# Batch 0's attention first and alone with filler matmuls, the weight fold behind tile 0

## Chip, cores, metric

One NeuronCore of one Trainium2 chip. The metric is device time in microseconds (us) of one execution; lower is better. Times quoted are medians of several runs, profiles are of one run each.

## The reference

Strided sparse attention over 8 batches, 8 heads, 576 positions, head size 64, then a feed-forward part without a nonlinearity:

```python
attn = softmax(mask(q @ k.T / 8)) @ v          # heads 0-3: local mask, 4-7: strided mask
x = attn.transpose(0, 2, 1, 3).reshape(4608, 512)
a = x @ w1;  b = x @ w2                         # 512 x 1024 each
out = ((a * b) @ w3) @ w_out                    # 1024 x 1024, 1024 x 512
```

There is no nonlinearity between w3 and w_out, so the kernel multiplies them once: w34 = w3 @ w_out, the **fold**. A **tile** is 512 tokens (nine of them), a batch is 576 tokens.

## The kernel before

Weights and q, k, v come as float32 through five 8 KB staging buffers (`stgp`) and are cast to float16 by POOL or ACT. Here the parts that matter, with cuts marked `...`:

```python
def load_w3(g, engs="pp"):
    st = stgp.tile([P, 2, DF], FP32, tag="stg")
    nc.sync.dma_start(st, ...)
    for i in range(2):
        t = ffn.tile([P, DF], FP16, tag="w3n", bufs=4)    # eight chunks, four buffers
        w3n[2 * g + i] = t
        copy(engs[i], t, st[:, i])

def load_vL(b):
    vt = v16L[b % 2]
    ...
    for pr in (bass.ds(32, 32), bass.ds(64, 64)):
        nc.gpsimd.tensor_copy(out=vt[pr, :, :, 0:D], in_=...)
    # the "shift copy": 32 partitions moved to another 32
    nc.vector.tensor_copy(out=vt[0:32, :, 1:LT, 0:D], in_=vt[96:P, :, 0:LT - 1, 0:D])

def fold_tr(jc): ...      # 8 transposes of one w3 chunk, copies by DVE and ACT
def fold_mm(jc): ...      # two halves of 4 matmuls each: one block of w34

# attention of batch b, pair p of heads, as a stream of short steps:
#   ph_T (transpose q, k)  ph_R (their remainders)  ph_S (scores, exp, mask)
#   ph_PV (times v, normalise)  ph_T2 (transpose back into xT)

def host(units, upto, lead=0):     # emit dense units, the stream's steps between them
    ...
```

```python
load_w3(0, "pa"); load_wo(0); load_wo(1); load_qk(0); load_rest(0)
load_w3(1); load_vL(0); load_w3(2); load_vS(0); load_w3(3)
load_w12(0); load_w12(1)
load_qk(1); ...                                   # batch 1
fold_tr(0)
host(fold, batch_end[0], lead=3)                  # fold hosts batch 0's attention
load_qk(2); ...
host(ab_halves(0), pos[0] + 8, lead=9)            # tile 0: a and b
host(o_halves(0), batch_end[1])                   # tile 0: out, hosts batch 1
for tch in range(1, 9): ...                       # tile t hosts batch t + 1
```

PE runs in the order written. On the other engines the framework's scheduler orders the instructions, and each then runs strictly in that order.

## Time and profile before

| | before |
|---|---|
| median of 4 runs | 301.46 us (300.86 to 304.81) |
| span of the profiled run | 302.7 us (that run took 304.5 us) |
| first scores of batch 0 | 29.2 us |
| tile 0's first b matmul | 53.6 us |
| tile 1's first matmul | 90.3 us |
| from there to the end | 212.4 us |

The last row is dense PE work (PE is busy for 206.2 of these 212.5 us). Nearly all the slack lies ahead of tile 1, so the table is read by its second to last row: whatever a change does in the loading, fold and tile 0 stages shows there. The profiled run was taken apart from the four and is as slow as the slowest of them, which matters when sums from the trace are added to the median.

One detail of that trace will matter. Batch 1's shift copy on DVE, and POOL's casts at that time (timeline of the kernel before; start, length, engine, line, operation, out and in, and in brackets the wait before it):

```profile
68.86 2.47 POOL L169 CAST t<-st 128x1024 f16<-128x1024 f32 x2 [2.47 <-DMA st<-in_k_dram]
...
70.45 1.22 DVE L186 COPY v16L<-v16L 32x1280 f16<-32x1280 f16 x1
71.27 0.87 POOL L177 CAST t<-st 128x512 f16<-128x512 f32 x1
```

### The profile page before, as it was taken

To read this page: it belongs to the slowest core of one execution; us is meant where nothing else is said; L and a number is where in the kernel's file an instruction comes from. 1 tells how busy PE (TensorE), PEld (TensorE's weight loads), DVE (VectorE), ACT (ScalarE), POOL (GpSimd) and SP (SyncE) were. 2 spreads that over 40 slices of the span, in tenths; PEclk is the share of its full clock that TensorE was granted. 3 is DMA by queue.
4 is the path that set the end of the run, shared out by engine and by line. 5 is a ranking of instruction groups with operands and counts; after the bars stand their busy time and mean duration, and the time that the engine had idled before them with its cause. 6 is when DMAs were issued, how large, how long until landed. Compare 5 with 4: busy or idle time off the path is not lost.

```text
span 302.7 us, 5967 instructions
## 1 busy us (share of the span) xinstructions
PE 271.2 (90%) x2401; PEld 142.3 (47%) x2401; DVE 168.1 (56%) x345; ACT 149.6 (49%) x272; POOL 96.2 (32%) x99
## 2 busy tenths in 40 slices
PE   1728887996889999999999999999999999999995
PEld 0305554343455455555555555555554555444442
DVE  1100776226777884887678568847755774340430
ACT  3414568263675546445555565555455444433332
POOL 4358525665235462656119306110000000000000
PEclk9975999799999999999999999999999999999999
DMA  7999999999189988999899460020012002002003
GB/s 256 361 292 267 342 382 268 186 292 144 38 266 223 208 216 214 345 168 226 226 207 287 132 167 2 2 106 35 1 38 106 0 2 104 35 2 111 28 2 140
DMA packets 55612, 48.63 MB, mean 161 GB/s; under 512 B 28192, under 2 KB 44576, under 8 KB 55584
## 3 DMA queue, kind: packets, MB, share of 16 engines
q1 hardware_dynamic: 50400, 38.80, 52.7%
q10 hardware_dynamic: 5184, 9.44, 8.8%
q8 instruction: 19, 0.31, 0.5%
q14 instruction: 9, 0.07, 0.1%
HBM read 38.80 MB, written 9.44 MB: 159 GB/s over the span
## 4 chain that ended last, share of the span: by engine, by line
PE 75%; ACT 8%; DVE 6%; SPq 4%; DMA 3%; issue 3%; POOL 0%; ACTq 0%
PE ops L339 22%; PE bps L325 20%; PE aps L316 18%; PE ps L218 5%; PE xps L272 5%; DVE ptm L259 3%; DMA st<-in_moe_w_dram 3%; PE sps L252 3%; ACT pte L257 3%; SPq L163 2%; SPq L175 2%; PE ps L288 2%; ACT xT L295 2%; ACT osb L350 1%; DVE kT L72 1%
## 5 line engine op out<-in xcount | busy, mean ns | idle before, releaser
L316 PE MATMUL aps<-xT,w1h 128*128 128x512 f16 x288 | 76.1, 382 | 2.5 <-ACT xT L295 2.3
L319 ACT COPY asb<-aps 128x512 f32<-128x512 f32 x72 | 42.2, 586 | 71.4 <-PE aps L316 70.0
L327 DVE TENSOR_TENSOR abt<-bps,asb 128x512 f16<-128x512 f32 x72 | 49.5, 687 | 49.1 <-PE bps L325 48.4
L325 PE MATMUL bps<-xT,w2h 128*128 128x512 f16 x288 | 74.9, 383 | 0.0
L339 PE MATMUL ops<-w,abt 128*128 128x512 f16 x288 | 70.7, 379 | 0.0
L169 POOL CAST t<-st 128x1024 f16<-128x1024 f32 x32 | 34.1, 1094 | 33.5 <-PE ps L218 14.7
L257 ACT ACTIVATE pte<-sps 128x576 f16<-128x576 f32 (+1 forms) x64 | 38.4, 650 | 6.7 <-PE sps L252 6.5
L280 DVE TENSOR_TENSOR xqs<-xps,rcp 96x384 f16<-96x384 f32 (+1 forms) x64 | 39.6, 619 | 2.0
L325 PEld LDWEIGHTS <-w2h 128*128 128x128 f16 x288 | 25.7, 98 | 30.3 <-issue 6.0
L350 ACT COPY osb<-ops 128x512 f32<-128x512 f32 x36 | 21.1, 586 | 31.6 <-PE ops L339 31.6
L70 ACT COPY qT<-ps 128x512 f16<-128x512 f16 (+1 forms) x48 | 22.9, 481 | 27.8 <-PE ps L218 21.8
L316 PEld LDWEIGHTS <-w1h 128*128 128x128 f16 x288 | 25.4, 98 | 22.8 <-issue 1.1
L339 PEld LDWEIGHTS <-abt 128*128 128x128 f16 x288 | 24.9, 98 | 23.4
L185 POOL CAST v16L<-st 32x1536 f16<-32x1536 f32 (+1 forms) x16 | 24.0, 1497 | 27.7 <-DMA st<-in_v_dram 17.8
L272 PEld LDWEIGHTS <-ptm 72*128 72x128 f16 (+1 forms) x448 | 21.2, 97 | 23.0 <-DVE ptm L259 9.3
L259 DVE TENSOR_TENSOR ptm<-pte,maskL 128x576 f16<-128x576 f16 x32 | 17.5, 548 | 16.1 <-ACT pte L257 15.6
L259 DVE TENSOR_TENSOR ptm<-pte,maskS 72x576 f16<-72x576 f16 x32 | 21.7, 687 | 8.5 <-ACT pte L257 8.3
L196 POOL CAST v16S<-st 72x1024 f16<-72x1024 f32 x16 | 17.1, 1083 | 25.7 <-PE xps L272 14.6
L72 DVE COPY kT<-ps 128x512 f16<-128x512 f16 (+1 forms) x36 | 18.8, 535 | 11.2 <-ACT qT L70 11.1
L339 PE MATMUL ops<-woh,w3T 128*128 128x512 f16 x64 | 20.4, 454 | 3.1 <-POOL woh L74 2.0
L218 PE MATMUL ps<-id,t 128*128 128x128 f16 x256 | 20.3, 223 | 2.8 <-POOL t L169 2.8
L218 PEld LDWEIGHTS <-t 128*128 128x128 f16 x256 | 17.1, 100 | 11.3 <-POOL t L169 3.3
(52 smaller groups left out, 185.4 us busy)
## 6 DMA issues: line engine op xcount, KB each, us to landing
out_dram<-osb ACTq DMA_DIRECT2D x36, 256.0 KB, 2.0
st<-in_moe_w_dram SPq DMA_DIRECT2D x8, 1024.0 KB, 12.1
st<-in_q_dram SPq DMA_DIRECT2D x8, 1024.0 KB, 8.9
st<-in_k_dram SPq DMA_DIRECT2D x8, 1024.0 KB, 13.4
st<-in_v_dram SPq DMA_DIRECT2D x8, 576.0 KB, 10.0
st<-in_v_dram SPq DMA_DIRECT2D x8, 512.0 KB, 10.4
st<-in_moe_w_out_dram SPq DMA_DIRECT2D x2, 1024.0 KB
st<-in_q_dram SPq DMA_DIRECT2D x8, 128.0 KB, 11.2
```

Source lines behind the costliest of these rows:

```text
L169: nc.gpsimd.tensor_copy(out=t, in_=sts[nm][:, 4 * grp:4 * grp + 4].rearrange("p h c d -> p c h d"))
L218: pe(nc.tensor.transpose(ps[:, i, c * P:(c + 1) * P], src[:, c, h0:h0 + 2].rearrange("p h d -> p (h d)"), id16))
L257: nc.scalar.activation(out=pte[0:kr], in_=sps[0:kr, :, 0:288], func=AF.Exp, bias=0.0, scale=scale)
L259: nc.vector.tensor_mul(ptm[0:kr, 0:576].rearrange("p (a x) -> p a x", x=w), pte[0:kr].rearrange("p h (a x) -> p (h a) x", x=w), _ap(mk, 0, ...
L272: pe(nc.tensor.matmul(xps[:, h, i * 65:(i + 1) * 65], ptm[0:kr, c0:c0 + P], vt[0:kr, 2 * (s.hp % 2) + h, g * m + i, :], start=True, stop=T ...
L280: nc.vector.tensor_mul(xqs[0:w, 0:m].rearrange("p i h d -> p h i d"), xv[:, :, :, 0:D], _ap(rcp, 0, [[rp, w], [4, 2], [1, m], [0, D]]))
L316: pe(nc.tensor.matmul(aps, w1h[:, ci, bass.ds(jc * P, P)], xT[ci][:, tok], start=(ci == 0), stop=(ci == KM - 1)))
L319: nc.scalar.copy(out=asb, in_=aps)
L325: pe(nc.tensor.matmul(bps, w2h[:, ci, bass.ds(jc * P, P)], xT[ci][:, tok], start=(ci == 0), stop=(ci == KM - 1)))
L327: nc.vector.tensor_mul(abts[tch][:, jc, :], bps, st["asb"])
L339: pe(nc.tensor.matmul(st["ps"], lhs(ci), rhs(ci), start=(ci == 0), stop=(ci == KF - 1)))
L350: nc.scalar.copy(out=osb, in_=ps)
```

## The change

Intent: let batch 0's attention, which needs only q, k, v, start as soon as they land, so that tile 0's a and b (dense work) start early; put the fold behind them, where it can host batch 1's attention. While batch 0's attention runs alone, two 512-column matmuls of an identity before each step ("filler") are to keep PE's clock up.

```diff
--- before.py
+++ after.py
@@ -156,7 +156,7 @@
 
     x16 = {}
 
-    def load_qk(b):
+    def load_qk(b, engs="pp"):
         sts = {}
         for nm, ten in (("q", q), ("k", k)):
             st = stgp.tile([P, H, 4, D], FP32, tag="stg")
@@ -164,9 +164,9 @@
                               ten[b, :, 0:NM].rearrange("h (p c) d -> p h (c d)", c=4))
             sts[nm] = st
         for grp in range(2):
-            for nm in "qk":
+            for nm, eng in zip("qk", engs):
                 t = qkp.tile([P, 4, 4, D], FP16, tag=f"{nm}{grp}")
-                nc.gpsimd.tensor_copy(out=t, in_=sts[nm][:, 4 * grp:4 * grp + 4].rearrange("p h c d -> p c h d"))
+                copy(eng, t, sts[nm][:, 4 * grp:4 * grp + 4].rearrange("p h c d -> p c h d"))
                 x16[(b, nm, grp)] = t
 
     def load_rest(b):
@@ -412,38 +412,44 @@
                 pos[0] += 1
 
 
+
+    def spin():
+        ps = psF.tile([P, NT], FP32, tag="f", name="spin")
+        for i in range(2):
+            pe(nc.tensor.matmul(ps, id16, _ap(id16, 0, [[id16.ap[0][0], P], [0, 4], [1, P]]),
+                                start=True, stop=True))
+
+    load_qk(0, "pa")
+    load_rest(0)
+    load_vL(0)
+    load_vS(0)
+    load_w12(0)
+    load_w12(1)
     load_w3(0, "pa")
     for g in range(2):
         load_wo(g)
-    load_qk(0)
-    load_rest(0)
-    load_w3(1)
-    load_vL(0)
-    load_w3(2)
-    load_vS(0)
-    load_w3(3)
-    load_w12(0)
-    load_w12(1)
+    for g in range(1, 4):
+        load_w3(g)
     load_qk(1)
     load_rest(1)
     load_vL(1)
     load_vS(1)
 
-    fold = []
-    fold_tr(0)
+    fold = [lambda: fold_tr(0)]
     for jc in range(KF):
         h0, h1 = fold_mm(jc)
         fold.append(h0)
         if jc + 1 < KF:
             fold.append(lambda jc=jc: fold_tr(jc + 1))
         fold.append(h1)
-    host(fold, batch_end[0], lead=3)
+    ALONE = batch_end[0]
+    host([spin] * ALONE, ALONE)
     load_qk(2)
     load_rest(2)
     load_vL(2)
     load_vS(2)
-    host(ab_halves(0), pos[0] + 8, lead=9)
-    host(o_halves(0), batch_end[1])
+    host(ab_halves(0) + fold[0:8], pos[0])
+    host(fold[8:] + o_halves(0), batch_end[1])
     for tch in range(1, NTILE):
         units = ab_halves(tch) + o_halves(tch)
         if tch + 1 < B:
```

> **What bounds the kernel now.** I read the busy times first, then a table of stretches, the chain that ended last, the PE timeline of the first 90 us, and the orders in which the changed kernel's instructions stand on each engine (from its build, without times).
>
> The page, parts 1 and 2 (busy tenths in 40 slices of 7.6 us):
>
> ```profile
> PE 271.2 (90%) x2401; PEld 142.3 (47%) x2401; DVE 168.1 (56%) x345; ACT 149.6 (49%) x272; POOL 96.2 (32%) x99
> PE   1728887996889999999999999999999999999995
> PEclk9975999799999999999999999999999999999999
> DMA  7999999999189988999899460020012002002003
> ```
>
> PE is 90% busy and full from slice 12 on. Only the first 90 us has slack, and there the DMA engines are full too. The table of stretches (window, length, busy us and instruction count of PE, PEld, DVE, ACT, POOL, clock, DMA share, GB/s) is cut where the stages change:
>
> ```profile
> 0.00:24.50 24.50, 9.19 (x47) 5.05 (x48) 2.90 (x16) 6.56 (x8) 12.07 (x24) 0.89 1.02 296
> 24.50:53.30 28.80, 24.16 (x265) 14.00 (x263) 16.61 (x34) 19.81 (x36) 15.62 (x15) 0.91 1.02 320
> 53.30:62.95 9.65, 9.65 (x38) 4.00 (x38) 2.77 (x4) 2.92 (x5) 6.66 (x7) 0.82 1.19 214
> 62.95:90.20 27.25, 21.93 (x264) 12.53 (x263) 17.43 (x34) 17.37 (x36) 11.65 (x10) 1.00 0.77 171
> 90.20:118.80 28.60, 27.98 (x279) 14.72 (x276) 22.09 (x43) 14.82 (x29) 14.71 (x14) 1.00 0.99 215
> ```
>
> Stages: loading; fold (w34 = w3 times w_out) with batch 0's attention between its units; tile 0's a/b alone; the rest of tile 0 with batch 1's attention; tile 1. Everything after tile 1's first matmul at 90.25 us is the same in both kernels, so **the question is only when tile 1 starts**. PE's idle in the last stage before it is 5.1 us on the timeline, the largest 2.2 us for v:
>
> ```profile
> 53.28 0.51 PE L316 MATMUL aps<-xT,w1h 128*128 128x512 f16 x1 [0.79 <-ACT xT L295]
> 53.58 1.91 PE L325 MATMUL bps<-xT,w2h 128*128 128x512 f16 x4
> ...
> 71.72 0.28 PE L272 MATMUL xps<-v16L,ptm 128*128 128x65 f16 x4 [2.21 <-DVE v16L L186]
> ```
>
> The chain of waits shows the pitch of a unit of four 512-column matmuls: 1.71 us at half clock, 0.86 us at full:
>
> ```profile
> 53.78 1.71 PE bps L325 x4
> 55.49 1.58 PE aps L316 x4
> 57.06 0.86 PE bps L325 x4
> 57.93 0.86 PE aps L316 x4
> ```
>
> **What the Trainium skill says.** (1) "TensorE: Matmul & The Clock Gate", Part 1: the array runs at half rate until about one 3.4 us window of activity has passed, and after an idle window falls back. The trace agrees: pitches 1.71 and 0.86 us per unit, the granted clock 0.50 from about 20 to 29 us and again at 54 to 56 us, each after a thin stretch. (2) The same page, Part 4, says that transposes do not count as activity; that would be why the change adds real matmuls as filler. No row here isolates it. (3) "SBUF — State Buffer", "Who interferes with whom": DVE copies in a two-port mode and GpSimd lock each other out. The trace agrees: the v16L copy (L186) took 0.49 us at 31.36 and 1.22 us at 70.45 while POOL was casting. (4) "DMA: Bandwidth & Descriptors", Specifications: transfers under 512 B miss line rate. Agrees: with 256-byte rows of q, k, v in flight the full engines moved about 180 GB/s (51 to 60 us), 350 or more with weights.
>
> **The change part by part.** *Removed:* no useful work; the fold (16 halves, 8 transposes) leaves batch 0's stage. *Added:* 42 filler matmuls, two before each of the 21 steps of batch 0's stream (the order on PE has 84 more rows: 42 weight loads and 42 matmuls). At the pitch above they cost 0.43 us a step warm, 0.86 cold. *Moved:* batch 0's data first, w1 and w2 next, then w3(0), w_out, the rest of w3; k's casts for batch 0 go to ACT.
>
> *Arrivals.* The first 1 MB load was cast at 5.93 us and the next at 8.83, 11.72, 14.73 and 18.08, so about 3 us per MB. So q is there at 6.1, k at 9.3, the remainder of q and k near 11, v near 14 and 16, w1/w2 halves from 19 to 28, w3 and w_out from 31 to 46. The bytes up to batch 1 are the same in both, so k of batch 1 lands near 53 us as before (cast at 53.20).
>
> *Batch 0's attention.* ACT casts k in two pieces of 1.04 us, to 11.4. The transposes share one PSUM buffer, so T, R, T run one after the other, each with its copies of 1.0 to 1.1 us: the first scores at **15.8 us** (before: 29.15). From the first scores to a0's last matmul took 24.1 us before (29.15 to 53.28). Per pair now: scores 0.45, two exps 1.2, mask 0.6, PV 0.4, reciprocal and scale 0.75, transposes and copies, with two score/PV buffers in rotation: about 4.5 to 5 us, PE's own share 2 us of stream plus 2.2 us of filler. To that come 1.5 us of waiting for v's casts (2 x 1.5 us on POOL, then the DVE copy), half clock at the start, and two pairs of w1 casts at 2.0 us, which stand in ACT's order between the copies of pair 3's q and k and between pair 3's two exps, squarely on the chain. I get 22.8 us: the fold was not what made this stage long, latency was. **a0 done at 38.6**, 14.7 us earlier than before.
>
> *Tile 0's a/b:* 15 units x 0.865 = 13.0, plus 1.7 for the clock cold again after ACT's casts: **53.3**. Then three fold transposes (0.45 each), five halves (0.865) and 0.5 for the first w3T copy: 6.2, to **59.5**.
>
> *Fold's rest and outputs over batch 1:* 11 halves 9.5, five transposes 2.25, eight output halves 6.9, batch 1's stream 10.0 (before: 27.25 us less 5.1 idle less 14 halves of 0.865). Sum 28.65. *Waits:* on POOL the cast of k of batch 1 stands behind the last w3 cast, which needs a buffer that the fourth fold transpose frees: it starts near 61.7 where PE wants it at 60, so 2.8 us lost with the cast itself. Then R, v16L and the exps, about 3.5 us (before 5.1). Tile 1 starts at 59.5 + 28.65 + 6.3 = **94.5 us, against 90.25: 4.2 us later**. The check from the other side: the fold's 16 x 0.865 + 8 x 0.45 + 0.5 = 17.9 us now stand behind a0, which gains only 14.7; that is +3.2, and +1.2 of extra waiting. From 301.54 this makes 305.7. Several of my waits may overlap, so I choose 305.0.
>
> **The rivals.** (a) *The stage alone is much shorter.* For it: ACT had 19.8 busy us and DVE 16.6 in the 28.8 us stretch, some 9 and 7 of them fold copies, now gone; pairs at 4 us would end a0 near 33, and tile 1 would start 5 us earlier than in my sum: 299 to 301. Against: the w1 casts and v's arrival remain. (b) *A wash through the loads.* Batch 1's k lands at 53 in both, v at 58 to 62; if PE waited for these, an earlier a0 would be worth nothing and a later one would cost nothing: 301 to 303. Against: PE still has dense work then. (c) *The filler does not hold the clock.* If the gaps at v and at ACT's casts leave it at 0.5, a pair costs PE 8 us, a0 comes at 44 or later: 310 to 314. For it: the clock fell at 20 and at 54 us after stretches with about 40 to 60% PE busy. Against: at half clock the filler itself makes PE nearly full, which warms it.
>
> **Range and chances.** Uncertain are a0 (2.5 us either way), the clock at a/b (1.5), the wait for k of batch 1 (1.5) and the rest of batch 1's waits (1.5): about 3.7 us together. So 305.0, with 300 to 311 eight times in ten, skewed up by (c). Faster by over 2% means under 295.5, which needs a0 before 29 us: 0.04. Slower by over 2% is over 307.6, 0.7 of that spread away: 0.25. Within 2%: 0.71.
>
> **What would show it.** Right: first scores at 15 to 17 us; a0 complete at 36 to 41; the clock low once more at the start of a/b; the first transpose of batch 1 waiting 2 to 3 us for POOL's cast; tile 1's first aps matmul at 92 to 97; tiles 1 to 8 as long as before (212 us). Wrong: a0 near 33 or below (the fold's copies had been the limit), or pairs of 8 us (cold), or idle PE in the a/b stage for w1 or w2.

## The result

The changed kernel took **316.36 us** (313.75 to 317.97, four runs) against 301.46: slower, ratio 1.046 (95% interval 1.036 to 1.057). A ratio here is the mean time of one kernel's fast runs over the mean of the other's fast runs of the same rounds, so not quite the ratio of the medians.

The page's busy tenths, changed kernel (40 slices of 7.9 us):

```profile
PE   2657799783998999999999999999999999999995
PEclk9989799978999999999999999999999999999999
```

Counted from 0, PE is now dense in slices 5 and 6, earlier than before, and then falls to 7, 8 and 3 in slices 7 to 9. The clock dips in slices 8 and 9. Stretches of the changed kernel, cut at its own stages (batch 0's attention; tile 0's a/b; the fold's first part; fold and outputs over batch 1; tile 1 to the end; the columns are as in the prediction):

```profile
0.00:40.68 40.68, 23.82 (x223) 12.00 (x224) 15.35 (x38) 18.89 (x31) 17.86 (x28) 0.92 0.98 289
40.68:53.63 12.95, 12.95 (x62) 5.88 (x61) 4.84 (x7) 7.51 (x11) 2.02 (x2) 1.00 1.04 346
53.63:60.84 7.21, 6.44 (x53) 3.73 (x52) 2.56 (x5) 2.24 (x4) 4.16 (x5) 1.00 1.16 165
60.84:100.17 39.33, 30.75 (x316) 18.05 (x317) 21.80 (x38) 19.46 (x40) 24.52 (x23) 0.91 0.76 180
100.17:314.80 214.63, 206.71 (x1798) 106.60 (x1794) 128.22 (x257) 103.83 (x189) 45.71 (x40) 1.00 0.44 113
```

Tile 0's b begins 12.9 us earlier (40.68 against 53.58), yet tile 1 begins 9.9 us later (100.17 against 90.25). The fourth stretch has 8.6 us of PE idle and a clock of 0.91. Its largest waits, on the PE timeline:

```profile
63.79 0.40 PE L218 MATMUL ps<-id,t 128*128 128x128 f16 x4 [2.56 <-POOL t L74]
...
65.73 1.91 PE L339 MATMUL ops<-woh,w3T 128*128 128x512 f16 x4
...
75.81 0.38 PE L272 MATMUL xps<-v16L,ptm 128*128 128x65 f16 x4 [4.74 <-DVE v16L L186]
76.00 1.90 PE L339 MATMUL ops<-woh,w3T 128*128 128x512 f16 x4
```

The second and the last line show the clock at half after each of the two waits: four matmuls in 1.91 and 1.90 us, where 1.03 would be usual. The granted clock read 0.50 from 65.7 to 67.4 us and again from 75.8 to 79.0. What DVE and POOL did then, from the timeline of the changed kernel:

```profile
58.76 5.96 POOL L74 CAST t<-st 128x1024 f16<-128x1024 f32 x6 [1.12 <-PE trp L361]
...
65.34 2.97 POOL L185 CAST v16L<-st 32x1536 f16<-32x1536 f32 x2
...
68.38 2.02 POOL L196 CAST v16S<-st 72x1024 f16<-72x1024 f32 x2
...
70.35 4.50 POOL L74 CAST t<-st 128x1024 f16<-128x1024 f32 x4
...
72.01 3.74 DVE L186 COPY v16L<-v16L 32x1280 f16<-32x1280 f16 x1
...
74.80 0.61 POOL L177 CAST t<-st 128x512 f16<-128x512 f32 x1
```

POOL works almost without a pause from 58.8 to 75.4 us: the last w3 chunks, whose buffers the fold's transposes free only now, then batch 1, then at once batch 2, whose q and k have landed meanwhile. The shift copy took 1.22 us before. It now takes 3.74 us and ends at 75.75, just after POOL's last cast. In the kernel before, POOL's casts came spaced by the arrival of their data.

### The profile page after: what moved, and what is told of

It is laid out like the page before. It is cut to its first block, busy times and chain, and to the rows that moved or that the text cites. A ratio compares the mean times of both kernels' runs of the same rounds, so it can differ in the third digit from the quotient of the medians.

```text
span 314.8 us, 6055 instructions
## 1 busy us (share of the span) xinstructions
PE 280.7 (89%) x2443; PEld 146.3 (46%) x2443; DVE 172.8 (55%) x345; ACT 151.9 (48%) x274; POOL 94.3 (30%) x97
## 4 chain that ended last, share of the span: by engine, by line
PE 74%; ACT 10%; DVE 8%; issue 3%; DMA 3%; POOL 1%; SPq 0%; ACTq 0%; POOLq 0%; DVEq 0%
PE ops L339 22%; PE bps L325 19%; PE aps L316 17%; PE xps L272 5%; PE ps L218 5%; DVE ptm L259 3%; ACT pte L257 3%; PE sps L252 3%; DMA st<-in_k_dram 3%; DVE v16L L186 2%; ACT xT L295 2%; PE ps L288 2%; PE spin L419 1%; ACT qT L70 1%; POOL t L74 1%
## 5 line engine op out<-in xcount | busy, mean ns | idle before, releaser
L316 PE MATMUL aps<-xT,w1h 128*128 128x512 f16 x288 | 75.3, 379 | 2.4 <-ACT xT L295 2.2
L325 PE MATMUL bps<-xT,w2h 128*128 128x512 f16 x288 | 74.0, 379 | 0.0
L74 POOL CAST t<-st 128x1024 f16<-128x1024 f32 x37 | 39.2, 1086 | 42.7 <-PE ps L218 17.3
L70 ACT COPY qT<-ps 128x512 f16<-128x512 f16 (+1 forms) x48 | 22.8, 481 | 34.9 <-PE ps L218 31.2
L272 PEld LDWEIGHTS <-ptm 72*128 72x128 f16 (+1 forms) x448 | 21.9, 99 | 31.3 <-DVE ptm L259 13.5
L259 DVE TENSOR_TENSOR ptm<-pte,maskL 128x576 f16<-128x576 f16 x32 | 19.2, 612 | 22.6 <-ACT pte L257 22.2
L218 PE MATMUL ps<-id,t 128*128 128x128 f16 x256 | 21.2, 228 | 8.6 <-POOL t L74 6.0
L259 DVE TENSOR_TENSOR ptm<-pte,maskS 72x576 f16<-72x576 f16 x32 | 20.9, 662 | 11.9 <-ACT pte L257 11.7
L278 DVE RECIPROCAL rcp<-xps 96x6 f32<-96x6 f32 (+1 forms) x64 | 12.2, 190 | 19.0 <-PE xps L272 18.9
```

The source lines that it names most:

```text
L70: nc.scalar.copy(out=out, in_=in_)
L74: nc.gpsimd.tensor_copy(out=out, in_=in_)
L218: pe(nc.tensor.transpose(ps[:, i, c * P:(c + 1) * P], src[:, c, h0:h0 + 2].rearrange("p h d -> p (h d)"), id16))
L259: nc.vector.tensor_mul(ptm[0:kr, 0:576].rearrange("p (a x) -> p a x", x=w), pte[0:kr].rearrange("p h (a x) -> p (h a) x", x=w), _ap(mk, 0, ...
L272: pe(nc.tensor.matmul(xps[:, h, i * 65:(i + 1) * 65], ptm[0:kr, c0:c0 + P], vt[0:kr, 2 * (s.hp % 2) + h, g * m + i, :], start=True, stop=T ...
L316: pe(nc.tensor.matmul(aps, w1h[:, ci, bass.ds(jc * P, P)], xT[ci][:, tok], start=(ci == 0), stop=(ci == KM - 1)))
```

## The experiments

**Theory A:** the loss comes from POOL. Its casts, bunched by the buffers, lock the DVE shift copy out, PE waits and cools; plus the fold's 17.9 us of PE work, which has lost its hiding place. **Theory B:** the order alone makes the kernel late, and the waits merely swap. **Rivals C and D:** the filler is needed for the clock, or is itself the cost. **E and F:** the long copy is chance, or slow for another reason. **G:** loads bound the start whatever the order.

| run | median us | ratio to before (95%) | tile 0's b | tile 1 |
|---|---|---|---|---|
| changed | 316.36 | 1.046 (1.036-1.057) | 40.7 | 100.2 |
| x0 changed again | 315.75 | 1.043 (1.036-1.049) | 41.0 | 101.5 |
| x1 shift copy on ACT | 312.24 | 1.035 (1.027-1.042) | 41.4 | 95.8 |
| x2 batch 2's casts on ACT | 316.02 | 1.042 (1.033-1.050) | 41.7 | 100.0 |
| x3 room for w3 | 309.06 | no verdict | 37.3 | 88.1 |
| x4 no filler | 312.09 | 1.031 (1.024-1.038) | 38.9 | 96.9 |
| x5 room, copy on ACT | 308.10 | 1.012 (1.001-1.023) | 37.1 | 87.7 |
| x5 again | 308.12 | 1.014 (1.005-1.022) | 39.8 | 92.0 |
| x7 as x5, no filler | 308.29 | 1.018 (1.012-1.023) | 38.5 | 91.6 |
| y1 before, copy on ACT | 303.35 | 0.999 (0.992-1.006) | 54.4 | 89.0 |
| z1 batch 0 first, fold hosts | 299.52 | 0.991 (0.985-0.997) | 50.9 | 86.3 |
| z2 as z1, 12 steps alone | 303.91 | 1.007 (0.999-1.014) | 55.8 | 93.6 |
| z3 as z1, 6 steps alone | 299.85 | 0.987 (0.982-0.992) | 53.2 | 87.2 |

The medians are over all runs, the ratios over fast runs only (two of four in x5, three of four in x5 again, x2 and y1). The kernel before ran beside all of them: 302.2 to 303.0 us median in the chip sessions of the experiments, single runs from 299.8 to 306.4. By the rule that a difference counts from 2% on, the changed kernel, x0, x1, x2 and x4 are slower, both x5 and x7 unclear, and y1 and the three z runs the same. The two last columns are from one profiled run each, which may be at either end of the spread; the ratios decide.

### x0: the changed kernel again

No edit.

> The changed kernel unaltered, for a second profile and as the reference on this chip. Theory A (lockout of the DVE shift copy by POOL's casts of batch 2): the copy takes 2.5 us or more again, PE waits 3 us or more for v16L, tile 1 starts at 98 to 101, 314 to 317. Rival E (the 3.74 us copy was a chance of that one trace and the slowdown comes from elsewhere): the copy takes 0.5 to 1.3 us and the time is still 314 to 317.

From its timeline:

```profile
41.00 1.91 PE L325 MATMUL bps<-xT,w2h 128*128 128x512 f16 x4
...
73.32 3.75 DVE L186 COPY v16L<-v16L 32x1280 f16<-32x1280 f16 x1
...
77.12 0.38 PE L272 MATMUL xps<-v16L,ptm 128*128 128x65 f16 x4 [4.74 <-DVE v16L L186]
```

The copy took 3.75 us, PE waited 4.74 us, and tile 1 came at 101.5, half a us past my range. Rival E falls: this is no accident of one trace. The first line shows what did differ: here tile 0's b began at half clock, with the same filler ahead of it.

### x1: the shift copy on ACT

```diff
-        nc.vector.tensor_copy(out=vt[0:32, :, 1:LT, 0:D], in_=vt[96:P, :, 0:LT - 1, 0:D])
+        copy("a" if b == 1 else "v", vt[0:32, :, 1:LT, 0:D], vt[96:P, :, 0:LT - 1, 0:D])
```

> Batch 1's partition-shift copy of v16L goes to ACT in place of DVE; nothing else changes. Theory A (the miss is the DVE copy locked out for 3.74 us while POOL casts batch 2, and the cold clock that follows): the copy takes 0.6 to 0.8 us on ACT, PE's wait for v16L falls from 4.74 us to about 1, no half clock at 76 us, tile 1's first matmul moves from 100.2 to 94 to 95, time about 310.5. Theory B (the order itself is late, one wait replaces another): the wait turns up elsewhere, 314 to 316.

From its timeline:

```profile
71.08 2.53 POOL L74 CAST t<-st 128x1024 f16<-128x1024 f32 x2
...
72.19 1.26 ACT L70 COPY v16L<-v16L 32x1280 f16<-32x1280 f16 x1
73.51 0.28 PE L272 MATMUL xps<-v16L,ptm 128*128 128x65 f16 x4 [1.71 <-ACT v16L L70]
```

With POOL casting at the same moment, ACT makes the copy in 1.26 us (I had expected 0.6 to 0.8), PE's wait falls from 4.74 to 1.71 us, and the matmuls after it run at full clock. Tile 1 starts at 95.8, the ratio falls from 1.046 and 1.043 to 1.035. The trace supports A: the one copy and what it drags along were late by about 3 us. The time alone does not show it, because the intervals overlap (1.027 to 1.042 against 1.036 to 1.049), and at 312.24 us it lies between my 310.5 and B's 314.

### x2: batch 2's casts on ACT, the copy left on DVE

```diff
-    load_qk(2)
+    load_qk(2, "aa")
```

> The changed kernel with batch 2's four q/k casts on ACT in place of POOL; batch 1's shift copy stays on DVE. Theory A (POOL's casts lock the DVE copy out): with POOL idle the copy takes about 0.5 us, PE's wait for v16L falls from 4.7 to 1.5 us, tile 1 starts at 95 to 98; ACT's 4 us of casts may give back part of it: 310 to 314. Rival F (the DVE copy is slow for another reason, such as its own data or DMA traffic): it takes 3 us or more again, 315 to 318.

From its timeline:

```profile
69.42 2.02 POOL L196 CAST v16S<-st 72x1024 f16<-72x1024 f32 x2
...
72.76 0.49 DVE L186 COPY v16L<-v16L 32x1280 f16<-32x1280 f16 x1
...
75.71 0.61 POOL L177 CAST t<-st 128x512 f16<-128x512 f32 x1 [4.28 <-DMA st<-in_k_dram]
...
84.96 0.41 PE L288 MATMUL ps<-id,xqs 96*128 96x96 f16 x6 [2.21 <-ACT kT L70]
```

The mechanism stands out: with POOL idle from 71.4 to 75.7 the same DVE copy takes 0.49 us. Rival F falls. But the time did not move (316.02 us, ratio 1.042, expected 310 to 314): the casts now sit in ACT's order at 79.6 to 84.4 us, PE waits 2.21 us for ACT's copy of k behind them, and tile 1 starts at 100.0. Taking the lockout away bought nothing where the casts went onto another engine of the same chain. This is Theory B in small, and so x2 says nothing on what the lockout costs in time.

### x3: room for all eight w3 chunks

The last four chunks go into columns of xT that batches 6 and 7 write much later.

```diff
-            t = ffn.tile([P, DF], FP16, tag="w3n", bufs=4)
+            if g < 2:
+                t = ffn.tile([P, DF], FP16, tag="w3n", bufs=4)
+            else:
+                t = xT[2 * g + i - 4][:, NTOK - DF:NTOK]
```

> The last four w3 chunks are cast into columns of xT not used until later, so no w3 cast waits for a fold transpose, and POOL casts batch 1's q, k and v as they land. Theory A: the 2.56 us wait for batch 1's k goes, v is cast some 4 us earlier, and the shift copy on DVE is less locked out (0.5 to 2 us): tile 1 at 92 to 95, time 307 to 311. Theory B: POOL's order does not matter, 314 to 316.

In its profile the wait for batch 1's k is gone, the copy takes 0.49 us, and tile 1 starts at 88.1, earlier than in the kernel before. But that run (303.17 us) is the only one of its four that counts as fast; the others, at 308.6 to 310.0 us and granted clocks of 0.978 to 0.989 against 0.998, count as slow. So there is no verdict on its time. It is part of x5, which has one.

### x4: no filler

```diff
-    host([spin] * ALONE, ALONE)
+    host([lambda: None] * ALONE, ALONE)
```

> The changed kernel without the 42 filler matmuls. Theory A (the stage alone is bound by the chain through ACT, DVE and POOL; filler is partly in series with it): b0 starts 1 to 2 us earlier than 40.7, but the a/b stage starts at half clock and gives 1.7 to 3 us back: 314 to 318. Rival C (the filler holds the clock and is needed): the stage runs at half clock throughout, 319 or more. Rival D (the filler is what makes the change slow): 311 or less.

From its PE timeline:

```profile
37.23 1.90 PE L316 MATMUL aps<-xT,w1h 128*128 128x512 f16 x4
38.93 1.91 PE L325 MATMUL bps<-xT,w2h 128*128 128x512 f16 x4
40.63 1.31 PE L316 MATMUL aps<-xT,w1h 128*128 128x512 f16 x4
```

And from the timelines of DVE, POOL and PE before its copy:

```profile
66.59 2.02 POOL L196 CAST v16S<-st 72x1024 f16<-72x1024 f32 x2
67.11 4.00 DVE L259 TENSOR_TENSOR ptm<-pte,maskL 128x576 f16<-128x576 f16 x2 [0.79 <-ACT pte L257]
68.55 2.24 POOL L74 CAST t<-st 128x1024 f16<-128x1024 f32 x2
69.95 0.24 PE L272 MATMUL xps<-v16L,ptm 128*128 128x65 f16 x2 [2.77 <-DVE ptm L259]
71.14 0.49 DVE L186 COPY v16L<-v16L 32x1280 f16<-32x1280 f16 x1
```

312.09 us, ratio 1.031: faster than my range for A, just slower than D's. Without filler the attention alone ends 1.8 us earlier (b at 38.9), then the a/b stage starts cold, as the 1.90 us per four matmuls show, and the first fold transpose comes at 53.0 against 53.6 us. So in this trace the filler itself is nearly neutral: it buys a warm a/b stage with about as much time as that is worth. Nor does it buy it every time: with filler the stage began warm in six of seven profiles (not in x0), without it in neither of two (x4, x7). Most of this run's gain appears later, in batch 1's stage. Its copy fell into a gap of POOL's casts and took 0.49 us, but that is not the gain: the casts met the two mask multiplies ahead of it instead, which took 4.00 us (0.51 and 0.46 in x2), and PE waited 2.77 us for the first. What the stage over batch 1 saved, 2.5 us against the changed kernel's trace, is half of it shorter PE work (29.6 us against 30.8) and half of it idle time, mostly shorter waits for batch 1's q and k. So it is not this one copy alone that is at risk beside a run of casts. Rival C (filler needed) falls.

### x5 and x5 again: room for w3 and the copy on ACT

Both edits of x1 and x3.

> Both edits together. Theory A: all waits on POOL in batch 1's stage gone or under 1 us each: tile 1 at 89 to 92 and 304 to 307, about the kernel before: what remains is the order of the work, which gains nothing. Theory B: 313 to 316.

> Room for all w3 chunks and the shift copy on ACT, a second time, because its runs spread from 304 to 311. If the spread is the clock (granted clock 1.0 in the fastest, 0.98 in the slowest), a profile with clock 0.98 shows tile 0's b0 at 40 or later in place of 37, and runs fall in two groups near 303 and 308. If the clock is not it, the time does not follow the clock column.

The second run's stretches, fold and outputs over batch 1, then tile 1 to the end:

```profile
59.75:92.00 32.25, 28.77 (x320) 17.45 (x318) 17.55 (x37) 20.75 (x41) 20.18 (x18) 0.95 0.96 218
92.00:306.30 214.30, 206.70 (x1797) 106.89 (x1793) 126.94 (x257) 103.76 (x189) 45.74 (x40) 1.00 0.44 112
```

Two sessions agree: 308.1 us, just above my 304 to 307, and ratios of 1.012 and 1.014, whose intervals are clear of the changed kernel's. The stage over batch 1 takes 32.3 us in place of 39.3, with 3.5 us of PE idle; the longest wait left is 2.07 us for the copy on ACT. So POOL's bunching, the casts held by the buffers and the lockout together, accounts for about 3 of the 4.4 per cent.

The source of the spread is not settled. The slow runs of both have clocks of 0.972 to 0.977; the first profile, at 1.00, had b at 37.1 and the second, at 0.989, at 39.8. That fits the clock, but there were not two groups as I had written, and a slow run at 0.976 (308.50 us) was no longer than a fast one at 0.994 (308.25). The traces show a rival. Mask multiplies of batch 0's second pair, in the changed kernel's profile and in x5's first:

```profile
23.70 2.14 DVE L259 TENSOR_TENSOR ptm<-pte,maskL 128x576 f16<-128x576 f16 x2 [2.22 <-ACT pte L257]
22.51 1.00 DVE L262 TENSOR_TENSOR ptm<-pte,maskL 128x576 f16<-128x576 f16 x2 [1.69 <-ACT pte L260]
```

Over the first three pairs they took 5.7 us in the changed kernel (b at 40.7), 5.0 in x5 again (39.8) and 3.3 in x5 and in x3 (37.1 and 37.3). How they fall beside POOL's casts may thus make the spread; no run isolates it.

### x7: as x5, without filler

> As x5, without the filler matmuls. Theory A (the stage alone is bound by the chain through ACT, DVE and POOL): 303 to 308, within 2 us of x5, with the a/b stage starting at half clock. Rival C (the filler is needed for the clock): 311 or more. Rival D (the filler costs time): 302 or less.

308.29 us, ratio 1.018 against 1.012 and 1.014, the intervals overlapping. With POOL's bunching gone, filler or no filler makes no difference that these runs can tell. Rival D (302 or less) falls too.

### y1: the kernel before with the copy on ACT

The edit of x1 on the kernel before.

> The kernel before with batch 1's shift copy on ACT. Its trace has a 2.2 us wait for the DVE copy there (1.22 us of copy). Theory A: the wait falls to about 1 us or less, 300 to 301.5. Theory B (the wait is replaced by another): no change, 302 to 303.

303.35 us, ratio 0.999. The 2.2 us wait became 1.1 us and tile 1 came at 89.0, but no difference in time shows; the interval (0.992 to 1.006) leaves room for the 1 to 2 us of Theory A. The copy took 1.27 us here, with POOL idle (between casts that ended at 67.6 and began at 70.8), as against 1.26 in x1 with POOL casting.

### z1, z2, z3: batch 0 first, but the fold still hosts it

One part of the change alone: batch 0 is loaded first, w3 and w_out second, w1 and w2 third. The first n steps of batch 0's attention run alone, then the fold hosts the rest as in the kernel before; no filler.

The edit, condensed (several statements to a line):

```diff
     load_qk(0, "pa"); load_rest(0); load_vL(0); load_vS(0)
+    load_w3(0, "pa"); load_wo(0); load_wo(1)
+    load_w3(1); load_w3(2); load_w3(3)
     load_w12(0); load_w12(1)
-    load_w3(0, "pa"); load_wo(0); load_wo(1); load_w3(1); load_w3(2); load_w3(3)
...
-    host([spin] * ALONE, ALONE)
+    while pos[0] < 8: stream[pos[0]](); pos[0] += 1      # z2: 12, z3: 6
+    fold_tr(0); host(fold[1:], batch_end[0])
...
-    host(ab_halves(0) + fold[0:8], pos[0])
-    host(fold[8:] + o_halves(0), batch_end[1])
+    host(ab_halves(0), pos[0] + 8, lead=9)
+    host(o_halves(0), batch_end[1])
```

> Only one part of the change: batch 0 loaded first with k cast on ACT, but w3 and w_out next and w1, w2 after them; no filler; the first 8 steps of batch 0's attention alone, then the fold hosts the other 13 as in the kernel before. Theory A (what is lost is the hiding place of the fold's 17.9 us; loading batch 0 first is good in itself): the fold is done and tile 0's b0 starts at 47 to 49 (before 53.6), when w1 and w2 have landed; tile 1 at 84 to 87; 295 to 299. Rival G (loads bound this part whatever the order): b0 at 52 to 54, 300 to 304.

> As z1 with 12 steps of batch 0's attention alone ahead of the fold. Theory A: within 2 us of z1, b0 at 47 to 50, since w1 and w2 land no earlier; 295 to 300. Rival G: 300 to 304.

> As z1 with 6 steps of batch 0's attention alone ahead of the fold (z1: 8, 0.991 of the kernel before; z2: 12, 1.007). Theory A (PE work that can hide behind batch 0's chain is what counts, and w3's first chunk lands near 19 us): the first fold transpose stands ahead of the third pair's transposes and the second scores and can start near 20.5 us (z1: 22.4), so b0 at 49 to 51 and a ratio of 0.985 to 0.993. Rival G (loads bound this part): same as z1 or, if the fold's first weights are waited for, 0.995 to 1.005.

Stretches of z1, tile 0's a/b before batch 1, then the rest of tile 0 over batch 1:

```profile
50.88:58.65 7.77, 7.77 (x38) 3.51 (x37) 2.77 (x4) 2.92 (x5) 3.06 (x5) 1.00 1.09 171
58.65:86.30 27.65, 23.53 (x266) 13.61 (x265) 16.12 (x34) 17.31 (x36) 16.57 (x15) 0.94 0.92 224
```

z1: 299.52 us, 0.991; z3: 299.85 us, 0.987 (five rounds). Both are **faster than the kernel before by about 1%**: a small gain, within 2%, but with intervals below 1, and so they beat both kernels. z1's b starts at 50.9 us, between my 47 to 49 and G's 52 to 54, and its time is just above my range. z2 missed: 303.91 us, b at 55.8. With 12 steps alone, more of the fold has to stand behind them: six and eight steps gain, twelve do not (0.999 to 1.014). z3's fold did not start at 20.5 us as I had written but at 22.0, after a wait of 2.16 us for POOL's cast of w3:

```profile
21.99 1.03 PE L361 MATMUL trp<-id,t 128*128 128x128 f16 x8 [2.16 <-POOL t L74]
```

Its b, at 53.2 in the one trace, is later than z1's, and its ratio is still where I expected it. That is luck: the way there was not the one I gave. Against the profile of the kernel before, z3's b comes only 0.4 us earlier. The gain lies behind it, 34.0 us from b to tile 1 against 36.7, with a and b warm from the start and a wait of 0.28 us for the shift copy in place of 2.21. Rival G is not out either: in both traces POOL's casts of w_out and w3 between 23 and 31 us each waited some 1.6 us for their loads.

z1 against x7 is the test of the order: both load batch 0 first, both are without filler. They differ in where w3 and w_out are loaded and the fold computed, in tile 0's a and b, which host eight steps of batch 1 in z1 and none in x7, and in x7's two mends, which help x7. 0.991 against 1.018: the place of the fold with its loads and this hosting is worth some 2.7% (1.0175 / 0.9908).

## Why the prediction was wrong

It had the sign and half of the mechanism (a fold of 17.9 us moved from under batch 0's chain to behind tile 0, against less than 15 us gained; measured were 12.9), but not the half that lies on POOL. It forecast 305.0 us, with 300 to 311 as the range. The time was 316.36.

- *First scores at 15.8 us:* right, 15.07 (16.0 in x0).
- *a0 done at 38.6:* 2.1 us short; b started at 40.68. Filler partly in series is one part (x4: 38.9). The mask multiplies of pairs 0 and 1, next to POOL's casts, took 1.88 and 2.14 us per pair in the trace where my sum has 0.6; x5's first profile, with 1.27 and 1.00, had b at 37.1, but no run isolates these. Batch 0's own shift copy, also next to POOL's casts, took 1.33 us (0.49 in the kernel before).
- *a/b stage to 53.3:* right in sum (53.63), by luck, with two misses: it started later, but warm. In x0 it began at half clock, as I had forecast.
- *Wait for k of batch 1, 2.8 us:* right, 2.56 (2.56 in x0 too).
- *"Then R, v16L and the exps, about 3.5 us (before 5.1)":* **the step that failed.** These waits were 6.0 us, 4.74 of them for v16L. I had named the lockout of DVE by POOL (point 3) and cited 1.22 us for it, and I had seen in POOL's order that the w3 casts would hold everything behind them. I did not join the two: casts held back come out in one run, and the copy waits for the whole run. The clock fell to half after this wait, and before that after the wait for k; the stage's granted clock was 0.91, and I had no term for it. Together the stage from 60.2 us on took 40.0 us against my 35.0: 2.5 us more of these waits, 2.7 us more of busy PE (31.4 against 28.65), 0.2 us less for k. The traces of x1 and x2 show the cause of the long wait. What held casts and lockout cost together x5 shows, some 3%; the share of the one copy is not clear of noise (x1).
- *"Everything after tile 1's first matmul is the same":* not quite, 214.6 against 212.4 us. Tile 1 took 29.4 us against 28.6 and tile 3 29.5 against 27.9, the latter with a mask multiply of 1.64 us beside POOL's cast of v. All profiles of the changed order have this tail of 213.4 to 214.6 us; the z runs, with the fold ahead, have 211.5 to 211.7. No run takes it apart, so its cause stays open.
- *From 301.54 plus the difference:* the difference was worked out on a profiled run of 304.5 us, 3 us above the median of the kernel before, and then added to the median. That left out some 3 us: the traces differ by 12.1 us, the medians by 14.9.
- *"About 180 GB/s (51 to 60 us)":* too low a reading; the whole stretch moved 207 GB/s, its lowest two us 169. The forecast does not rest on it.

The terms on the traces: I had 4.2; the a0 step adds 2.1, the middle stages some -1.4, batch 1's stage 5.0, the tail 2.2, in sum 12.1. Of the rivals, (a) and (b) fell. (c) is half right. The clock fell to half twice in batch 0's stage in spite of the filler (0.50 from 22.0 to 24.4 us, 0.54 from 31.6 to 34.9), but a0 came at 40.7 and not at 44; and it fell twice over batch 1, where there is no filler, after the waits for k and v16L.

What remains of the loss in x5 and x7, 1.2 to 1.8%, I put down to the fold's place; z1 and z3 make that likely. Not all of it is accounted for so: in x5 again about 2 us of some 4 come after tile 1's start (214.3 us against 212.4), in the tail left open above. How much of it is the fold's PE time and how much the later arrival of w3 isn't separated. Nor is the spread of x3 settled.

## What to carry to other kernels

Filler matmuls are worth little where real work could stand in their place: the gap behind batch 0's chain was the fold's hiding place, and giving that up cost some 2.7% (z1 against x7). When an engine's instructions are held back by a buffer, ask what they will come out beside: here a run of casts on POOL stopped a small DVE copy until the run was over (3.74 us), and PE behind it. And take a part of a change on its own: batch 0 loaded first with the fold still beside its attention gained 1%, with the fold behind tile 0 it lost (1.8% in x7).

## What the Trainium skill lacked or had wrong

- "SBUF — State Buffer", "SBUF: two separate sides", says that GpSimd or a DVE operation in a two-port mode, whichever starts first, holds the shared port pair for the whole instruction and the other fully blocks. The runs agree, and show more than it says: the block can last over several casts in a row. A DVE copy of 0.49 us (x2, x3, x4, POOL idle when it began) took 3.74 and 3.75 us next to a run of five casts that began before it, and ended only after the last. Next to a run of three, in the kernel before (1.22 us) and in z2 (1.21 us), it ended inside the third. The page gives no bound for this, and why the cases differ stays open.
- The same page has PE and ACT never waiting for others at their ports. The runs agree for ACT: the copy took 1.26 us with POOL casting (x1) and 1.27 us with POOL idle (y1).
- "TensorE: Matmul & The Clock Gate", Part 1, warns that the clock's events in a trace can be unreliable. Agreed: in x4 the granted clock reads 1.00 from 37.2 to 41.0 us, while four matmuls take 1.70 us from start to start, twice the warm pitch. The pitch decides.
